# Threshold attention and a tanh-shrink layer on one core: all later k and q turned by the DMA crossbar, loads issued by ScalarE

## The chip, the core and the metric

The kernel runs on one core of a Trainium2 chip. The metric is the device time of one execution in microseconds (us), as the median over several runs. The core has a matrix engine (TensorE, PE in the profile, with its weight loads as PEld), VectorE (DVE), ScalarE (ACT), GpSimd (POOL) and a sync engine (SP) that only issues DMAs. Each of them works through its own instruction stream in order, and they wait for each other by semaphores. Sixteen DMA engines move the data; SP and ACT can both hand work to them. A DMA can also transpose 2-byte data on its way ("crossbar transpose").

## The reference

Attention over 8 batches x 8 heads, 576 rows of 64 numbers each; scores that lie more than `tau` below their row's maximum are dropped. A two-layer block follows, without a bias:

```python
scores = (1 / sqrt(64)) * q @ k.T                 # per batch and head, 576 x 576
thresh = max(scores, -1) - tau
scores = where(scores >= thresh, scores, -1e9)
attn = exp(scores - max(scores)); attn /= sum(attn) + 1e-9
x = (attn @ v), heads side by side                # 4608 x 512
h = x @ w_in                                      # 4608 x 2048
out = (h - tanh(h)) @ w_out                       # 4608 x 512, float32
```

## The kernel before

**Tiling.** Two heads of one batch make a pair; there are 32 pairs, four to a batch. A pair has nine score tiles of 128 query rows by 576 keys: four for each head and a ninth that holds the last 64 rows of both heads. So there are 288 tiles. The main loop runs over slots `s`, one tile wide: in slot `s` the scores of tile `s + 8` are made (AHEAD is 8), the threshold step `kink` is made for tile `s + 5`, the exponentials (`weights`) for tile `s`, and the product with v (`attend`) for tile `s - 2`.

**Preparing k and q.** q and k arrive in float32 (`load`, L137 to L153: a 256 KB piece for rows 0 to 511 of both heads, and a 32 KB piece for the last 64 rows, both on SP). POOL's `split` (L189 to L193) scales them and writes a high and a low fp16 half side by side, `hl`. These must be turned so that the 64 numbers of a row stand on the partitions: `turn` (L252). On PE that is nine transposes (L240) into one buffer of the two-buffer PSUM pool `ps_big`, which the scores also use, and one copy by DVE to `kT` or `qT` (L268). From pair 8 on, q of three pairs out of four goes another way: one crossbar transpose, issued by SP (L257), writes `qT` directly. For k, POOL then copies the two halves of the partitions into each other's place, `kS` (L274). The scores are sums of products with `kT` and with `kS` (L336; L327 for the shared ninth tile). `MAIN` and `REM` name the columns of a head's 512 first and 64 last keys.

**From the scores on.** DVE scales them out of PSUM and takes the row maximum (L346, L358); ACT makes the thresholded difference `z` (L373). In the first six pairs PE transposes z and ACT takes the exponentials from PSUM (L392, L401); from then on SP has z of two tiles turned by the crossbar (L380) and ACT takes the exponentials of both at once (L409). PE multiplies with v (L432, L439, L450), DVE divides, PE turns the result into `xT` (L482, L488, copied by L495 and L496).

**The second block.** When a batch's four pairs are through, its 512-row block goes through the two layers while the next batch's attention runs. An `h` step is four matmuls into `psH` (L505), then tanh on ACT (L518) and the difference on DVE (L524). A `y` step is four matmuls into `psY` (L531); every fourth one is copied out by DVE (L544) and stored by SP (L547). Which slot has an `h`, a `y` or nothing is written by hand in a string of 36 characters per batch, `PATTERN`, with 16 `h`, 16 `y` and four empty slots in the middle batches. The last 64 rows of all batches are gathered in `xR` and done in the end, after the attention.

**What sets the order.** The order is written out by hand. Each preparing step of pair `p` is put a number of slots ahead of the slot in which the pair's first scores are made:

```python
first = TPP * p - AHEAD                     # TPP = 9 tiles a pair
plan.setdefault(first - d, []).append(...)  # d: slots ahead
```

In before, k, q and v of a middle pair are loaded some 12 to 17 slots ahead, k is split 8 and q 7 to 10 slots ahead, k is turned 6 slots ahead, and q 6 or 7 by the crossbar and 2 by PE. Within a slot the plan's steps come last. Raw buffers, `hl`, `kT`, `qT` and `kS` have two copies each, so a step also waits until the pair two before it no longer needs its buffer.

Of the kernel before, what the change touches and what calls it, by code (L numbers as in the profile page):

```python
# [9 lines left out]
F32 = mybir.dt.float32  # L10
BF16 = mybir.dt.bfloat16
FP16 = mybir.dt.float16
# [6 lines left out]
def kernel(  # L19
# [11 lines left out]
    nc = tc.nc  # L31
    P = 128
# [13 lines left out]
    HPAIR = H // 2  # L46
# [85 lines left out]


    raws = {}

    def load(p, t):
        b, h0 = p // HPAIR, 2 * (p % HPAIR)
        hs = slice(h0, h0 + 2)  # L140
        src = {"k": k, "q": q, "v": v}[t]
        eng = nc.sync
        r = raws[p, t] = raw_pool.tile([P, 10, D], F32, name=f"{t}raw", tag=t)
        n = 8 if t == "v" else 10
        eng.dma_start(
            out=r[:, 0:n, :].rearrange("p (h c) d -> p h (c d)", h=2)[:, :, 0 : 4 * D],
            in_=src[b, hs, 0:512, :].rearrange("h (p c) d -> p h (c d)", c=4),
        )
        rem = src[b, hs, 512:S, :].rearrange("h s d -> s h d")
        if t == "v":  # L150
            eng.dma_start(out=r[0:64, 8:10, :], in_=rem)
        else:
            eng.dma_start(out=r[:, 4, :], in_=rem)  # L153

    def load_first(t, h, eng):

        src = {"k": k, "q": q}[t]
        if (0, t) not in raws:
            raws[0, t] = raw_pool.tile([P, 10, D], F32, name=f"{t}raw", tag=t)
        r = raws[0, t]  # L160
        if h is None:
            rem = src[0, 0:2, 512:S, :].rearrange("h s d -> s h d")
            eng.dma_start(out=r[:, 4, :], in_=rem)
        else:
            eng.dma_start(
                out=r[:, 5 * h : 5 * h + 4, :].rearrange("p c d -> p (c d)"),
                in_=src[0, h, 0:512, :].rearrange("(p c) d -> p (c d)", c=4),
            )
# [17 lines left out]
    def split(p, t):  # L186
        x = raws.pop((p, t))[:, 0:9, :]
        hl = hl_pool.tile([P, TPP, 2, D], FP16, name=f"{t}hl", tag=t)
        nc.gpsimd.tensor_scalar(  # L189
            out=x, in0=x, scalar1=QKSC, scalar2=1.0, op0=ALU.mult, op1=ALU.mult  # L190
        )
        nc.gpsimd.tensor_copy(out=hl[:, :, 0, :], in_=x)
        nc.gpsimd.tensor_tensor(  # L193
            out=hl[:, :, 1, :], in0=x, in1=hl[:, :, 0, :], op=ALU.subtract
        )
        hls[p, t] = hl
# [21 lines left out]

    def split_v(p):
        r, vb = raws.pop((p, "v")), vbs[p % NV]  # L220
        nc.gpsimd.tensor_copy(
            out=vb[:, :, 0:4, 0:D],
            in_=r[:, 0:8, :].rearrange("p (h c) d -> p h c d", h=2),
        )
        nc.gpsimd.tensor_copy(out=vb[0:64, :, 4, 0:D], in_=r[0:64, 8:10, :])
        nc.gpsimd.tensor_copy(out=vb[64:P, :, 5, 0:D], in_=r[0:64, 8:10, :])

    mats = {}  # L230


    by_head = lambda ap: ap.rearrange("p (s h) -> p h s", h=2)
    in_heads = lambda ap: ap.rearrange("p (h s) -> p h s", h=2)

    def turn_chunk(out, c, lhsT):
        rhs = ident_f16
        if c == 4:
            out, rhs = in_heads(out), by_head(rhs)
        nc.tensor.matmul(  # L240
            out=out, lhsT=lhsT, rhs=rhs, is_transpose=True, start=True, stop=True
        )
# [5 lines left out]

    def q_by_dma(p):

        return p >= 2 * HPAIR and p % 4 != 0

    def turn(p, t):
        hl = hls.pop((p, t))
        if t == "q" and q_by_dma(p):
            m = mats[p, t] = qk_pool.tile([P, W], FP16, name=f"{t}T", tag=t)
            nc.sync.dma_start_transpose(  # L257
                out=m.rearrange("p (c r) -> p c r", c=TPP),
                in_=hl.rearrange("p c a d -> p (c a d)"),
            )  # L260
            return
        ps = ps_big.tile([P, W], FP16, name=f"ps_{t}", tag="big")
        for c in range(TPP):
            turn_chunk(
                ps[:, c * P : (c + 1) * P], c, hl[:, c, :, :].rearrange("p a d -> p (a d)")
            )
        m = qk_pool.tile([P, W], FP16, name=f"{t}T", tag=t)
        nc.vector.tensor_copy(out=m, in_=ps)  # L268
        mats[p, t] = m
        if t == "k":  # L270
            sw = qk_pool.tile([P, W], FP16, name="kS", tag="ks")
            for lo, hi in ((0, D), (D, 0)):
                o, i = sw[lo : lo + D, :], m[hi : hi + D, :]
                nc.gpsimd.tensor_copy(out=o, in_=i)  # L274
            mats[p, "ks"] = sw

    def turn_first(t, part):

        hl = hls[0, t[0]]
        c0, c1 = ((0, 5), (5, TPP))[part]  # L280
        pl, tag = (ps_y, "y") if t == "ks" else (ps_h, "h")
        ps = pl.tile([P, 5 * P], FP16, name=f"ps1_{t}", tag=tag)
        for c in range(c0, c1):
            o = ps[:, (c - c0) * P : (c - c0 + 1) * P]
            if t == "ks":
                for a in range(2):
                    turn_chunk(o[64 * a : 64 * a + 64, :], c, hl[:, c, 1 - a, :])
            else:
                turn_chunk(o, c, hl[:, c, :, :].rearrange("p a d -> p (a d)"))
        if part == 0:  # L290
            mats[0, t] = qk_pool.tile([P, W], FP16, name=f"{t}T", tag=t)
        dst, n = mats[0, t][:, c0 * P : c1 * P], (c1 - c0) * P
        if part == 1 or t == "q":
            nc.scalar.copy(out=dst, in_=ps[:, 0:n])
        else:
            nc.vector.tensor_copy(out=dst, in_=ps[:, 0:n])


    MAIN = (slice(0, 512), slice(640, W))
    REM = (slice(512, 576), slice(576, 640))  # L300
    scs, mxs, nbs, zs, zts, pts, ops = {}, {}, {}, {}, {}, {}, {}

    def kind(i):
# [9 lines left out]
    def scores(i):  # L313
        p, hh, t = place(i)
        qT, kT, kS = mats[p, "q"], mats[p, "k"], mats[p, "ks"]
        ps = ps_big.tile([P, 1024], F32, name="psS", tag="big")
        main, rem, lo = slice(0, 512), slice(512, 576), 0
        if kind(i) == "B":
            main, rem, lo = slice(512, 1024), slice(448, 512), 448
        if hh is None:  # L320
            qrem = REM
            if q_by_dma(p):
                qrem = (slice(512, 640, 2), slice(513, 640, 2))
            for n, kk in enumerate((kT, kS)):
                for dst, srcs in ((main, MAIN), (rem, REM)):
                    for hh in range(2):
                        nc.tensor.matmul(  # L327
                            out=ps[64 * hh : 64 * hh + 64, dst],
                            lhsT=qT[:, qrem[hh]], rhs=kk[:, srcs[hh]],
                            start=(n == 0), stop=(n == 1),  # L330
                        )
        else:
            lhs = qT[:, (5 * hh + t) * P : (5 * hh + t + 1) * P]
            for n, kk in enumerate((kT, kS)):
                for dst, src in ((main, MAIN[hh]), (rem, REM[hh])):
                    nc.tensor.matmul(  # L336
                        out=ps[:, dst], lhsT=lhs, rhs=kk[:, src],
                        start=(n == 0), stop=(n == 1),
                    )
        sc = sc_pool.tile([P, S], F32, name="sc")  # L340
        if kind(i) == "B":
            mx = mxs[i] = mxs.pop(i - 1)
        else:
            mx = mxs[i] = mx3[i // 2 % len(mx3)]
        c = int(kind(i) == "B")
        nc.vector.tensor_scalar(  # L346
            out=sc, in0=ps[:, lo : lo + S], scalar1=SC, scalar2=None,
            op0=ALU.mult, op1=ALU.max, accum_out=mx[:, c : c + 1],
        )
        scs[i] = sc  # L350
# [163 lines left out]
    def bend():  # L514
        while halves:
            m, n, ps = halves.pop(0)
            th = t_pool.tile([P, MB], F32, name="th")
            nc.scalar.activation(out=th, in_=ps, func=ACT.Tanh)  # L518
            ths.append((m, n, ps, th))

# [8 lines left out]
    def project(m, ms, part, ps, last, cols=slice(0, d_model)):  # L529
# [4 lines left out]
            )  # L534
        if part == 3:
            nc_ = cols.stop - cols.start
            yo = y_pool.tile(
                [P, nc_], F32, name="yo", tag="yo" if nc_ == d_model else f"yo{int(last)}",
                bufs=2 if nc_ == d_model else 1,
            )  # L540
            if last:
                nc.scalar.copy(out=yo, in_=ps)
            else:
# [16 lines left out]
    EARLY = lambda m: 3 if m else 3  # L560
    LAST = 1

    PATTERN = lambda m: '-h--h-hh--h-hh-h-hh-h--hh-h--hh-y-yy' if m == 0 else 'hyhyhyhyhyhyhyhyhyhyhyhyhyhyhyhy' if m == B - 2 else 'yhyhyyy-yhyhhyyhy-hhhyhh-hyhyhy-yhhy'

    FIRST = 3
    quarters = lambda m: [(m, ms, part) for ms in range(4) for part in range(4)]
# [112 lines left out]
    )  # L679

    plan = {}
    for p in range(1, NPAIR):
        first = TPP * p - AHEAD
        for d, f in PREP[3 if p == 1 else 0 :]:
            d -= p == 1 and d == 3
# [150 lines left out]
```

## Time and profile before

| what | value |
|---|---|
| median of 9 runs | 518.06 us (518.0 to 518.22) |
| the profiled execution | 518.0 us, its span 516.2 us |
| PE busy | 501.7 us (97% of the span) |
| ACT busy | 433.0 us (84%) |
| DVE busy | 419.2 us (81%) |
| POOL busy | 289.9 us (56%) |
| DMA moved | 86.79 MB, mean 168 GB/s |
| crossbar transposes | 117 of z, 18 of q |

"Busy" is the time in which an engine works on an instruction; issuing DMAs and waiting don't count. The span runs from the first to the last instruction of the profiled execution, and the time of that execution is 1.8 us longer than the span. A share over the whole span mixes three stages: up to about 115 us (start, the first pairs, weights being loaded), the long middle up to about 421 us in which attention and layers run side by side, and an end of layers alone. The slices of the page show them, each digit the busy share of one fortieth of the span in tenths:

```profile
PE   8999899889999999999999999999999999999997
...
ACT  5999999999899989998999989998999899543430
...
DMA  6852669899998999999999998999979976311013
```

### The profile page before, as it was taken

How to read it: one execution, taken by the hardware profiler on the slowest of the kernel's cores; microseconds unless marked ns; L12 is line 12 of the kernel's file. 1: busy time of each engine (PE TensorE's matmuls, PEld its weight loads, DVE VectorE, ACT ScalarE, POOL GpSimd, SP SyncE). 2: the span in 40 equal slices, each digit the busy share in tenths (PEclk: the TensorE clock that was granted, in tenths of full speed). 3: DMA queues.
4: the chain of work that ended last, by engine and by line, in shares of the span. 5: the costliest groups of instructions: out<-in, count | busy, mean ns of one | idle time of the engine just before them, and what ended most of it. 6: DMA issues, size and time to landing. Idle time of an engine off the chain costs nothing.

```text
span 516.2 us, 12692 instructions
## 1 busy us (share of the span) xinstructions
PE 501.7 (97%) x4606; PEld 284.8 (55%) x4606; DVE 419.2 (81%) x1179; ACT 433.0 (84%) x617; POOL 289.9 (56%) x390
## 2 busy tenths in 40 slices
PE   8999899889999999999999999999999999999997
PEld 4666566555555555555555555555555555544444
DVE  5899889998899988998899888998999887644440
ACT  5999999999899989998999989998999899543430
POOL 7999999776565656566666656566656620000000
PEclk9999999999999999999999999999999999999999
DMA  6852669899998999999999998999979976311013
GB/s 213 252 151 90 208 194 230 162 189 187 200 197 172 210 207 199 177 192 215 209 164 200 202 206 195 185 200 207 204 162 194 174 140 116 98 41 42 20 43 82
DMA packets 208607, 86.79 MB, mean 168 GB/s; under 512 B 176160, under 2 KB 200992, under 8 KB 208544
## 3 DMA queue, kind: packets, MB, share of 16 engines
q1 hardware_dynamic: 207952, 85.56, 78.9%
q8 instruction: 36, 0.59, 0.5%
q10 hardware_dynamic: 592, 0.43, 0.3%
q14 instruction: 27, 0.22, 0.1%
HBM read 36.70 MB, written 9.44 MB: 89 GB/s over the span
## 4 chain that ended last, share of the span: by engine, by line
PE 79%; POOL 10%; ACT 3%; DVE 3%; issue 2%; DMA 1%; SPq 0%; POOLq 0%; ACTq 0%; DVEq 0%
PE psY L531 23%; PE psH L505 20%; PE psS L336 18%; PE psO L439 5%; PE psS L327 3%; PE psHt L505 3%; PE ps_k L240 2%; POOL kS L274 2%; POOL w_in_sb L655 1%; PE psO L450 1%; POOL khl L193 1%; PE psO L432 1%; DVE sc L346 1%; PE psX L482 1%; ACT z L373 1%
## 5 line engine op out<-in xcount | busy, mean ns | idle before, releaser
L373 ACT ACTIVATE z<-sc,nb 128x576 bf16<-128x576 f32 x288 | 217.7, 770 | 23.5 <-DVE nb L358 21.6
L346 DVE TENSOR_SCALAR_CACHE_REDUCE sc<-psS 128x576 f32<-128x576 f32 x288 | 213.5, 751 | 17.6 <-PE psS L336 13.5
L531 PE MATMUL psY<-w_out_sb,g 128*128 128x512 bf16 (+1 forms) x592 | 145.7, 373 | 0.0
L409 ACT ACTIVATE pT<-zT 128x1152 f16<-128x1152 bf16 x117 | 134.8, 1152 | 1.9 <-DMA zT<-z 1.6
L274 POOL COPY kS<-kT 64x1152 f16<-64x1152 f16 x62 | 70.7, 1141 | 109.6 <-DVE nb L358 58.4
L505 PE MATMUL psH<-xT,w_in_sb 128*128 128x512 bf16 x480 | 123.4, 379 | 1.0 <-DVE g L524 0.6
L336 PE MATMUL psS<-kT,qT 128*128 128x512 f16 (+1 forms) x512 | 104.4, 285 | 4.5 <-DVE sc L346 2.4
L336 PEld LDWEIGHTS <-qT 128*128 128x128 f16 x1024 | 72.9, 97 | 56.5 <-issue 5.3
L524 DVE SCALAR_TENSOR_TENSOR g<-th,psH 128x512 bf16<-128x512 f32 x128 | 87.4, 683 | 18.3 <-ACT th L518 18.0
L336 PE MATMUL psS<-kS,qT 128*128 128x512 f16 x496 | 101.4, 286 | 0.0
L518 ACT ACTIVATE th<-psH 128x512 f32<-128x512 f32 x128 | 74.6, 583 | 20.9 <-PE psH L505 20.9
L531 PEld LDWEIGHTS <-g 128*128 128x128 bf16 x592 | 51.1, 98 | 54.1 <-DVE g L524 0.4
L505 PEld LDWEIGHTS <-w_in_sb 128*128 128x128 bf16 x576 | 49.0, 98 | 56.3 <-issue 3.4
L439 PE MATMUL psO<-vb,pT 128*128 128x65 bf16 x1024 | 53.3, 194 | 0.0
L439 PEld LDWEIGHTS <-pT 128*128 128x128 f16 x1024 | 44.2, 98 | 9.4
L193 POOL TENSOR_TENSOR khl<-kraw,khl 128x576 f16<-128x576 f32 x31 | 39.7, 1280 | 2.7
L193 POOL TENSOR_TENSOR qhl<-qraw,qhl 128x576 f16<-128x576 f32 x31 | 39.7, 1280 | 2.7
L401 ACT ACTIVATE pT<-psZ 128x512 f16<-128x512 bf16 (+1 forms) x54 | 35.1, 653 | 2.8 <-PE psZ L392 2.5
L544 DVE COPY yo<-psY 128x512 f32<-128x512 f32 (+1 forms) x31 | 21.1, 681 | 14.7 <-PE psY L531 13.8
L465 DVE TENSOR_TENSOR osb<-psO,rc 128x256 bf16<-128x256 f32 x64 | 27.2, 424 | 2.2
L432 PE MATMUL psO<-vb,pT 128*128 128x130 bf16 x128 | 28.1, 220 | 0.0
L268 DVE COPY kT<-ps_k 128x1152 f16<-128x1152 f16 x31 | 23.4, 755 | 4.5 <-PE ps_k L240 4.3
(79 smaller groups left out, 508.4 us busy)
## 6 DMA issues: line engine op xcount, KB each, us to landing
vraw<-in_v_dram SPq DMA_DIRECT2D x32, 256.0 KB, 3.5
out_dram<-yo SPq DMA_DIRECT2D x32, 256.0 KB, 2.9
kraw<-in_k_dram SPq DMA_DIRECT2D x31, 256.0 KB, 3.3
qraw<-in_q_dram SPq DMA_DIRECT2D x31, 256.0 KB, 3.5
wt<-in_moe_w_in_dram SPq DMA_DIRECT2D x8, 512.0 KB, 4.4
wt<-in_moe_w_out_dram SPq DMA_DIRECT2D x8, 512.0 KB, 4.3
zT<-z SPq DMA_TRANSPOSE x117, 3.6
qraw<-in_q_dram SPq DMA_DIRECT2D x32, 32.0 KB, 3.1
```

The lines of the kernel that those rows point to most:

```text
L193: nc.gpsimd.tensor_tensor(out=hl[:, :, 1, :], in0=x, in1=hl[:, :, 0, :], op=ALU.subtract)
L274: nc.gpsimd.tensor_copy(out=o, in_=i)
L336: nc.tensor.matmul(out=ps[:, dst], lhsT=lhs, rhs=kk[:, src], start=(n == 0), stop=(n == 1),)
L346: nc.vector.tensor_scalar(out=sc, in0=ps[:, lo : lo + S], scalar1=SC, scalar2=None, op0=ALU.mult, op1=ALU.max, accum_out=mx[:, c : c + 1],)
L373: nc.scalar.activation(out=z, in_=sc, func=ACT.Prelu, bias=nb, scale=1.0, alpha=STEEP)
L401: nc.scalar.activation(out=pt[:, off * P : (off + n) * P], in_=ps[:, 0 : n * P], func=ACT.Exp)
L409: nc.scalar.activation(out=pt[:, 0 : n * P], in_=zts.pop(i)[:, 0:n, :], func=ACT.Exp)
L439: nc.tensor.matmul(out=po[:, t - 1 + ab, :], lhsT=pt[:, blk * P : (blk + 1) * P], rhs=vb[:, hh, c, :], start=False, stop=(n == 7), skip_gr ...
L505: nc.tensor.matmul(out=ps, lhsT=w_in_sb[:, c, n * P : (n + 1) * P], rhs=xs[m][:, c, :] if m < B else xR[:, c, :, :], start=(c == 0), stop= ...
L518: nc.scalar.activation(out=th, in_=ps, func=ACT.Tanh)
L524: nc.vector.scalar_tensor_tensor(out=gs[m][:, n, :], in0=th, scalar=-1.0, in1=ps, op0=ALU.mult, op1=ALU.add,)
L531: nc.tensor.matmul(out=ps, lhsT=gs[m][:, n, ms * P : (ms + 1) * P], rhs=w_out_sb[:, n, cols], start=(n == 0), stop=(n == DF_C - 1),)
```

## The change

From pair 8 on (`DUAL = 8`):

- **Turning.** k and q of every pair are turned by a crossbar transpose on SP (`q_by_dma`, `k_by_dma`). Before, PE turned every k, and q of every fourth pair. `kS` is still made by POOL, now in a step of its own, `swap`.
- **Loading.** `load_part` loads k in one DMA of 128 x 2304 bytes, in which a partition holds nine neighbouring rows of one head (partitions 0 to 63 the first head, 64 to 127 the second). q and v take two DMAs each: q as before in a 256 KB and a 32 KB piece, v in two halves by partitions, nine neighbouring rows to a pair of partitions. The five DMAs are issued by ScalarE, spread over slots.
- **Keys in another order.** As a chunk of turned k now holds 64 keys of each head, `main_keys` and `rem_keys` pick one head's keys in runs of 64 columns; v is put in the same order.
- **Timing.** For these pairs the table `LATER` gives the slots ahead of each step: `k0`, `q0`, `v0`, `q1`, `v1` are the loads, `s` the splits, `t` the turns, `kw` the swap. Even and odd pairs have different numbers.
- **Layer pattern.** The middle batches have a new string with the same 16 `h`, 16 `y` and four empty slots.
- **Buffers.** A raw tile is twice as wide (for an option of loading two pairs at once, which `AT_ONCE = 1` leaves unused); two small output tiles at the end share the tanh buffers.

```diff
+    DUAL = 8
+    AT_ONCE = 1
+    LOADER = nc.scalar
...
+    def load_part(p, t, part):
...
+        if t == "k":
+            dst = both[:, :, 0:TPP, :].rearrange("p a c d -> p a (c d)")
+            rows = rows.rearrange("(a h) s d -> a (h s) d", h=2).rearrange(
+                "a (p c) d -> p a (c d)", c=TPP
+            )
+        elif t == "v":
+            rows = rows.rearrange("h (p c) d -> p h (c d)", c=TPP)
+            if part == 0:
+                dst, rows = heads[0:64, :, 0 : 4 * D], rows[:, :, 0 : 4 * D]
+            else:
+                dst, rows = heads[64:P, :, :], rows[:, :, 4 * D :]
+        elif part == 0:
+            dst = heads[:, :, 0 : 4 * D]
+            rows = rows[:, 0:512, :].rearrange("h (p c) d -> p h (c d)", c=4)
+        else:
+            dst = both[:, part - 1, 4, :]
+            rows = rows[2 * part - 2 : 2 * part, 512:S, :].rearrange("h s d -> s h d")
+        LOADER.dma_start(out=dst, in_=rows)
...
     def q_by_dma(p):
 
-        return p >= 2 * HPAIR and p % 4 != 0
+        return p >= DUAL
+
+    def k_by_dma(p):
+        return p >= DUAL
 
     def turn(p, t):
         hl = hls.pop((p, t))
-        if t == "q" and q_by_dma(p):
-            m = mats[p, t] = qk_pool.tile([P, W], FP16, name=f"{t}T", tag=t)
+        if (q_by_dma if t == "q" else k_by_dma)(p):
+            m = mats[p, t] = qk_tile(t)
             nc.sync.dma_start_transpose(
-                out=m.rearrange("p (c r) -> p c r", c=TPP),
+                out=m[:, 0:W].rearrange("p (c r) -> p c r", c=TPP),
                 in_=hl.rearrange("p c a d -> p (c a d)"),
             )
             return
...
+    def swap(p):
+        m = mats[p, "k"]
+        sw = qk_tile("ks")
+        for lo, hi in ((0, D), (D, 0)):
+            o, i = sw[lo : lo + D, 0:W], m[hi : hi + D, 0:W]
+            nc.gpsimd.tensor_copy(out=o, in_=i)
+        mats[p, "ks"] = sw
...
+    def main_keys(p, kk, hh):
+        if p < DUAL:
+            return kk[:, MAIN[hh]]
+
+        return kk[:, 0 : 8 * P].rearrange("p (a n r) -> p n a r", a=2, n=4)[
+            :, :, :, 64 * hh : 64 * hh + 64
+        ]
...
-    PATTERN = lambda m: '-h--h-hh--h-hh-h-hh-h--hh-h--hh-y-yy' if m == 0 else 'hyhyhyhyhyhyhyhyhyhyhyhyhyhyhyhy' if m == B - 2 else 'yhyhyyy-yhyhhyyhy-hhhyhh-hyhyhy-yhhy'
+    PATTERN = lambda m: {
+        0: '-h--h-hh--h-hh-h-hh-h--hh-h--hh-y-yy',
+        B - 2: 'hyhyhyhyhyhyhyhyhyhyhyhyhyhyhyhy',
+    }.get(m, 'h-yhyhhyhyyhyyhh-yhhyhhy-yhyyh-yyhhy')
...
+    LATER = {
+        0: (
+            ("k0", 17), ("q0", 15), ("v0", 13), ("kt", 7), ("q1", 15),
+            ("ks", 8), ("v1", 12), ("vs", 6), ("qs", 10), ("qt", 7),
+            ("kw", 3),
+        ),
+        1: (
+            ("k0", 19), ("v1", 14), ("q0", 18), ("v0", 16), ("qs", 11),
+            ("q1", 17), ("qt", 8), ("ks", 13), ("vs", 6), ("kt", 10),
+            ("kw", 7),
+        ),
+    }
+    for p in range(DUAL, NPAIR):
+        first = TPP * p - AHEAD
+        at = lambda d, f: plan.setdefault(first - d, []).append(f)
```

## The prediction

> **What bounds the kernel now.** I read the page first (busy shares, slices, DMA issues), then busy time per stretch, then the chain of waits inside one stretch, then the waits, and last the timeline around ACT's DMAs.
>
> The stretch table is the central view: one row per two pairs (18 score tiles, start of one shared tile to the start of the next but one), with columns length, then busy time of PE, PEld, DVE, ACT, POOL, clock, DMA share and GB/s.
>
> ```profile
> core 0: us, PE busy (x) PEld busy (x) DVE busy (x) ACT busy (x) POOL busy (x), PEclk, DMA share, GB/s
> ...
> 197.80:225.00 27.20, 27.17 (x261) 15.47 (x260) 25.23 (x71) 25.61 (x36) 16.37 (x22) 1.00 1.02 195
> 225.00:253.40 28.40, 28.40 (x261) 15.85 (x262) 24.77 (x74) 26.17 (x36) 18.10 (x24) 1.00 1.01 201
> ...
> 421.00:444.00 23.00, 22.41 (x196) 12.21 (x197) 17.22 (x49) 20.97 (x29) 0.00 (x0) 1.00 0.62 125
> ```
>
> From 114.6 to 391.8 us there are ten such rows, 27.72 us each on average. PE is never idle in them, ACT is busy 25.77 on average (its ten rows lie between 25.36 and 26.17), DVE about 25.0. So PE sets the pace and ACT has only 1.95 us of room. The chain of waits in one stretch (start, length, what) says the same, and prices the work to be removed:
>
> ```profile
> 230.70 0.49 PE psS L336 x4
> 231.19 0.86 PE psY L531 x4
> 232.05 0.50 PE ps_k L240 x9
> 232.56 0.49 PE psS L336 x4
> ```
>
> Turning one k or q on PE is nine transposes in 0.50 us of the chain. (The group's busy time, 0.67, overlaps its neighbours; I use the chain's.) In this stretch every piece of the chain is PE. Who waits for what, from 197.8 to 308.9 us:
>
> ```profile
> ACT z L373 <- DVE nb L358: 6.7, 12, 0.8
> DVE sc L346 <- PE psS L336: 2.7, 4, 0.7
> ...
> ACT pT L409 <- DMA zT<-z: 0.4, 1, 0.4
> ```
>
> ACT waits for scores that PE has not yet made, 1.7 us per two pairs, and hardly ever for a crossbar transpose. The DMA issues of the same stretch (us to landing at the end):
>
> ```profile
> kraw<-in_k_dram SPq DMA_DIRECT2D x8, 256.0 KB, 3.0
> ...
> zT<-z SPq DMA_TRANSPOSE x37, 3.6
> ...
> qT<-qhl SPq DMA_TRANSPOSE x6, 3.4
> ```
>
> and, from the start of the kernel, the only mid-size loads that ACT issues:
>
> ```profile
> 0.73 0.65 ACTq L163 DMA_DIRECT2D kraw<-in_k_dram  x1
> ...
> 1.42 1.16 ACTq L165 DMA_DIRECT2D qraw<-in_q_dram  x2
> ```
>
> 0.58 to 0.65 us of ACT's instruction stream for each, while SP issued its own beside them.
>
> [...] No run here has large loads on ACT beside transposes. [...] The start of the trace shows two issuers at once with only about 0.1 us added (0.65 and 0.67 for 32 KB loads against a median of 0.565 on SP alone); beside a transpose it is not shown. [...]
>
> **The change, part by part.**
>
> *Turns leave PE and DVE.* For pairs 8 to 31, all 24 k turns and the 6 q turns that PE still did (every fourth pair) go: 30 x 0.50 = 15.0 us of PE chain. The changed program has 540 fewer PE instructions, which is 270 transposes with their weight loads. With them go 30 DVE copies of 755 ns, 22.7 us, 1.9 per two pairs, on an engine that was not the bound. Their two-buffer PSUM pool is then the scores' alone, which can only help. Per two pairs PE loses 2 k and half a q: 2.5 x 0.50 = 1.25, so its floor is 27.72 - 1.25 = 26.47.
>
> *What is late next.* ACT, with 25.77 of 26.47, 97%. DVE falls to about 23.1. Two engines that close, each in order and feeding the other, don't both run full: bounds are nothing lost (15.0 gained) and ACT keeping two thirds of its old idle time (1.3 us, so 27.07 per two pairs and 0.65 x 12 = 7.8 gained). I take a loss of 0.25 per two pairs: 1.0 x 12 = 12 us. After 426 us the chain already runs through ACT, which is a reason not to take the whole 15.
>
> *Transposes on SP.* 30 more, so 13 instead of 10.5 per two pairs. SP's issue time was 10.5 x 1.41 (median of zT) + 12 loads x 0.56 + 2 stores x 0.54 = 22.6 of 27.7; it becomes 13 x 1.41 + 1.1 = 19.4 of 26.5. So SP has more room. Its in-order waits are new: a kT or qT waits for POOL's split and the last reader of the buffer, and behind it stand zT transposes that ACT's exp waits for. By the plan, splits come one to three slots ahead and POOL has time to run ahead (16 to 18 us busy of 27.7). An odd pair's k and q each fall between two zT; an even pair's fall in one slot, and 3 x 1.41 = 4.2 us of issue meets two slots of 2.9 us, so the next zT is 1.3 us late. zT is asked for five slots after its input, about 7.3 us, and lands in 3.6: covered by about 2.4 us. Cost nothing; if landing grew by 3 us the cover would be gone and ACT would stall on it.
>
> *kS on POOL.* The swap (two copies of 1.14 us) now waits for a landed transpose rather than DVE. Even pairs: transpose 7 slots, swap 3 slots before the first score; 4 slots are 5.9 us against 3.4 to landing plus up to 2.8 of queue. Done about 1.4 slots ahead; nothing, with a few tenths a pair at risk.
>
> *Loads on ACT.* [...] They write buffers that POOL freed at least eight slots before, and most follow an activation of 0.77 to 1.15 us. [...] I take nothing; the lower bound is nothing too, because ACT issues almost none now, and the upper bound is all of it.
>
> *DMA traffic.* 2.5 more transposes per two pairs; k goes from 1 KB runs to 2.3 KB ones. The share of 1.0 looks full, but it goes above 1.0 in some stretches, so it counts packets that wait for each other; landing times near their minimum (zT 3.2 minimum, 3.6 median) say there is room. Cost nothing.
>
> *Moving operand in 64-column runs* (keys of both heads interleaved), and the *new layer pattern* (still 16 h, 16 y, 4 empty slots): same column counts. Strided reads by PE are not in the trace at this width; I take nothing, bound 10% below.
>
> **Sum.** Against the profiled execution, 518.0 us (span 516.2): 518.0 - 12 = 506.0, and the runs' median, 518.06, is 0.06 from it. Predicted 506, its own range 501 to 512.
>
> **Rivals.**
> - *ACT pays for its issues* (the slower side). Place: ACT's stream, pairs 8 to 31. Price: 5.7 us per two pairs times the exposed part. It decides from 1.95 / 5.7 = 34% exposed, where ACT alone needs the old 27.72. At half exposed: 25.77 + 2.85 = 28.62, 0.9 x 12 = 11 longer: 529. [...] Chance 0.19.
> - *DMA becomes the bound.* If 1.0 means full, 2.5 x 1.41 = 3.5 us more per two pairs, less about 1 for longer runs: 30 us longer, 548; half of that 533. Against: landings near their minimum. 0.08.
> - *Strided keys slow the score matmuls.* A score tile is the four matmuls of 0.49 us in the chain: 24 pairs x 9 tiles x 0.49 = 106 us; 8% slower costs 8: 514. For it: never run before. Against: the runs are whole 128-byte pieces. 0.10.
> - *No visible change* because ACT's room is less than it looks: 0.03.
>
> **Numbers.** Likeliest 0.60. Two per mille, 1 us, is what a measurement here can tell. Faster: 0.60 + most of the strided case, 0.69; same 0.04; slower 0.27. Range 500 to 527 leaves out a little below and the deeper half of the slow cases.
>
> **What would show it.** Right: no PE transposes after pair 7, two-pair stretches near 26.7 us, ACT above 95% busy, exp waiting for zT hardly more than now, ACT's DMA issues beside running activations. Wrong: ACT idle with "issue" or with a load ahead of it; zT landing at 6 us or more with ACT waiting; x4 score groups above 0.49 in the chain; PE waiting for kS.

## The result, and the profile after

| what | before | after |
|---|---|---|
| runs | 518.0 to 518.22 us, median 518.06 (31) | 508.9 to 521.73 us, median 513.48 (10) |
| the profiled execution | 518.0 us, span 516.2 | 508.9 us, span 507.1 |
| PE instructions, DVE instructions | 4606, 1179 | 4336, 1149 |
| zT, from issue to landing, min/median/max | 3.2 / 3.6 / 5.9 us | 3.2 / 4.6 / 8.8 us |

The change makes the kernel faster: the ratio is 0.9873 (0.9859 to 0.9887 at 95%), which stands for 518.06 x 0.9873 = 511.5 us. That ratio leaves out the four of the ten executions that were over 1.5% above the fastest, though the kernel before had none of that kind; with them in, the mean is 514.8 us. Two things came out of it: a gain of about 6.6 us by the ratio (3.2 by the mean of all ten), and a time that no longer repeats. The runs before lie within 0.2 us of each other, those after within 13.

The page of the kernel after: busy time by engine, DMA by slice, two of the queues (packets, MB, share of 16 engines' time), the chain that ended last, and the loads that ScalarE now issues (KB, us to landing).

```profile
PE 488.7 (96%) x4336; PEld 270.3 (53%) x4336; DVE 399.2 (79%) x1149; ACT 432.2 (85%) x617; POOL 291.1 (57%) x390
...
DMA  7852658999999999999999999999999976211013
...
q1 hardware_dynamic: 213520, 73.17, 75.1%
q10 hardware_dynamic: 20944, 21.67, 16.5%
...
PE 60%; POOL 11%; DMA 9%; ACT 7%; DVE 6%; issue 4%; ACTq 1%; SPq 1%; POOLq 0%
...
kraw<-in_k_dram ACTq DMA_DIRECT2D x24, 288.0 KB, 4.7
```

The fifth of these lines, the chain that ended last, is the one to read first. The same line of the kernel before:

```profile
PE 79%; POOL 10%; ACT 3%; DVE 3%; issue 2%; DMA 1%; SPq 0%; POOLq 0%; ACTq 0%; DVEq 0%
```

PE's own work has become shorter, as intended, and pieces of DMA, ACT and DVE now stand in the chain between its instructions. The 20,944 packets on the second queue, q10, are ScalarE's loads.

The stretch table again, four stretches of two pairs each (columns as before: length, busy time of PE, PEld, DVE, ACT, POOL, clock, DMA share, GB/s).

```profile
166.00:193.70 27.70, 27.43 (x243) 14.79 (x242) 23.76 (x70) 27.34 (x38) 19.25 (x25) 1.00 1.19 244
193.70:220.90 27.20, 26.11 (x235) 14.04 (x234) 22.61 (x67) 24.05 (x34) 15.89 (x21) 1.00 1.23 214
220.90:249.80 28.90, 28.14 (x243) 14.97 (x244) 24.12 (x72) 26.98 (x37) 17.85 (x23) 1.00 1.20 220
249.80:275.70 25.90, 25.82 (x234) 14.07 (x234) 22.91 (x68) 25.08 (x36) 17.58 (x23) 1.00 1.20 244
```

The ten stretches of the long middle last 27.3, 25.6, 27.7, 27.2, 28.9, 25.9, 27.3, 26.4, 28.5 and 25.6 us. Those without a stall alternate between 27.3 and 25.6, a mean of 26.45. The others run up to 1.6 us over: in the second row above PE is idle for 1.1 of 27.2 us and ACT for 3.2. The last columns changed too: the DMA share, 1.01 and 1.02 in the two rows of the middle shown before, is 1.19 to 1.23.

Who waits for whom in the whole span of the kernel after (us in total, times, longest):

```profile
POOL kS L323 <- DMA kT<-khl: 51.6, 15, 5.2
...
ACT pT L469 <- DMA zT<-z: 10.2, 11, 2.5
...
POOL kraw L225 <- DMA kraw<-in_k_dram: 6.0, 5, 2.2
```

ACT's wait for zT over the whole span of the kernel before:

```profile
ACT pT L409 <- DMA zT<-z: 1.6, 3, 0.9
```

The first line of the three above looks worst and is mostly harmless: POOL's swap waited for k before the change as well, 49.6 us in 12 times, and POOL has time.

One such stall close up, in the timeline (start, us, what; "x3" of the first row is three issues in a row, 9.00 us from the first's start to the last's end; the bracket is the engine's idle time and its releaser):

```profile
219.61 9.00 SPq L440 DMA_TRANSPOSE zT<-z  x3
...
219.90 0.76 ACT L433 ACTIVATE z<-sc,nb 128x576 bf16<-128x576 f32 x1
...
220.07 0.39 ACTq L172 DMA_DIRECT2D kraw<-in_k_dram  x1
...
227.90 0.67 POOL L225 TENSOR_SCALAR kraw<-kraw 128x576 f32<-128x576 f32 x1 [2.16 <-DMA kraw<-in_k_dram]
228.05 1.16 ACT L469 ACTIVATE pT<-zT 128x1152 f16<-128x1152 bf16 x1 [1.35 <-DMA zT<-z]
```

ScalarE issues a load of k at 220.07, beside an activation of its own that runs from 219.90 to 220.66: the issue, 0.39 us, costs ACT nothing, as its next activation starts at 220.57. The transfer takes 7.68 us in the chain of waits. In the same 9 us SP gets no more than three transposes issued, in 2.1, 3.0 and 3.1 us where the median is 1.45. At the end POOL has stood 2.16 us for k, and ACT 1.35 us for zT. Neither of these two engines was short of time. What their transfers have in common are the 16 DMA engines; whether those are what ran short, the experiments have to tell.

### The profile page after: what moved, and what is told of

The parts are those of the page before. It is cut to its first block, busy times and chain, and to the rows that moved or that the text cites. A ratio compares the mean times of both kernels' runs of the same rounds, so it can differ in the third digit from the quotient of the medians.

```text
span 507.1 us, 12208 instructions
## 1 busy us (share of the span) xinstructions
PE 488.7 (96%) x4336; PEld 270.3 (53%) x4336; DVE 399.2 (79%) x1149; ACT 432.2 (85%) x617; POOL 291.1 (57%) x390
## 2 busy tenths in 40 slices
DMA packets 234525, 95.61 MB, mean 189 GB/s; under 512 B 205152, under 2 KB 223840, under 8 KB 234464
## 3 DMA queue, kind: packets, MB, share of 16 engines
q10 hardware_dynamic: 20944, 21.67, 16.5%
## 4 chain that ended last, share of the span: by engine, by line
PE 60%; POOL 11%; DMA 9%; ACT 7%; DVE 6%; issue 4%; ACTq 1%; SPq 1%; POOLq 0%
PE psY L591 20%; PE psH L565 15%; PE psS L396 13%; DMA zT<-z 4%; PE psO L499 3%; ACT z L433 3%; POOL kS L323 3%; PE psHt L565 3%; DVE g L584 3%; ACT pT L469 2%; DVE sc L406 2%; DMA kraw<-in_k_dram 2%; ACT th L578 2%; PE psS L387 2%; POOL w_in_sb L717 1%
## 5 line engine op out<-in xcount | busy, mean ns | idle before, releaser
L469 ACT ACTIVATE pT<-zT 128x1152 f16<-128x1152 bf16 x117 | 135.2, 1156 | 10.8 <-DMA zT<-z 10.2
L396 PE MATMUL psS<-kS,qT 128*128 128x512 f16 (+1 forms) x512 | 104.6, 286 | 0.3 <-POOL kS L323 0.3
L525 DVE TENSOR_TENSOR osb<-psO,rc 128x256 bf16<-128x256 f32 x64 | 27.2, 424 | 2.2
L225 POOL TENSOR_SCALAR qraw<-qraw 128x576 f32<-128x576 f32 x31 | 20.8, 670 | 10.5 <-DMA qraw<-in_q_dram 8.9
```

The costliest lines, as they stand in the source:

```text
L396: nc.tensor.matmul(out=ps[:, dst], lhsT=lhs, rhs=cols(p, kk, hh), start=(n == 0), stop=(n == 1),)
L469: nc.scalar.activation(out=pt[:, 0 : n * P], in_=zts.pop(i)[:, 0:n, :], func=ACT.Exp)
```

## The experiments

The gain could have fallen short of the 15.0 us of PE time in four ways: ACT pays for its issues; two nearly full engines rub against each other, which is what the forecast had taken; transposes and loads crowd the DMA engines; or the lateness is one of order, and more slack cures it. Diffs are against the kernel after. Ratios are to the kernel before.

**The same issues with less to move.** All 120 loads of ScalarE stay where they are; from pair 10 on each moves about a quarter of its bytes, q's last rows apart, into raw tiles of its own. What isn't loaded is left from earlier pairs, and POOL's scaling there multiplies by 1.

```diff
+        if p >= DUAL + 2 and t == "k":
+            dst, rows = dst[:, :, 0 : 2 * D], rows[:, :, 0 : 2 * D]
+        elif p >= DUAL + 2 and (t == "v" or part == 0):
+            dst, rows = dst[:, :, 0:D], rows[:, :, 0:D]
```

> The changed kernel with the same 120 DMA issues on ACT, but from pair 10 on k, q and v loads move only about a quarter of the bytes (k 2 of 9 chunks, q and v one of four or five); the rest of the data is left from earlier pairs. Traffic theory (loads and transposes crowd the 16 DMA engines, so transposes land late and exp waits): runs near 504 to 506 us, lying within about 1 us of each other instead of 13, zT landing back to 3.6 to 4.0 us median, exp's wait for zT under 3 us. Issue theory (ACT pays for issuing loads): no change, about 511 with the same scatter. Close-engines theory (PE and ACT at 97% disturb each other): no change.

Measured: median 503.45 us (502.64 to 505.0), ratio 0.9719 (0.9706 to 0.9732). Two stretches of it, and the landing of zT:

```profile
141.60:167.20 25.60, 25.28 (x231) 13.99 (x234) 23.09 (x68) 24.73 (x35) 18.54 (x25) 1.00 0.98 179
167.20:194.50 27.30, 26.98 (x239) 14.75 (x242) 23.77 (x70) 26.70 (x37) 18.04 (x23) 1.00 1.07 182
```

```profile
DMA to landing us min/median/max: 3.2/3.5/8.4
```

Between 141 and 273 us its chain of waits is PE's again, with 1.2% for anything else:

```profile
by line: PE psS L404 29.7%; PE psH L573 25.8%; PE psY L599 25.7%; PE psO L507 7.7%; PE psS L395 4.2%; PE psO L518 2.2%; PE psO L500 1.7%; PE psX L550 1.7%; issue 1.2%; PE psX L556 0.2%
```

This run settles two theories at once. 14.6 of the 15.0 us come through with every issue of ScalarE in place, so the issues cost next to nothing. And they come through with ACT 97 to 98% busy (24.73 of 25.60, 26.70 of 27.30), so these two nearly full engines didn't rub. Only bytes were taken away, and the loss went with them. The trace has as many DMA packets as that of the kernel after, 234,525, so it isn't their number.

**Fewer transposes, full loads.** The same question from the other side: two of nine crossbar transposes of z in every two pairs are left out.

```diff
+            if DUAL * TPP <= i and i % 18 in (1, 11):
+                zts[i] = zt_last[0]
+                return
```

> The changed kernel with two of the nine zT transposes of every two pairs left out from pair 8 on (those tiles' exponentials read the zT turned before); PE, ACT, DVE, POOL and all loads do what they did. By uncontended packet times the DMA engines are asked for 23.1 of 26.45 us per two pairs in the changed kernel, 20.1 in the run with short loads, 20.2 of 27.7 before, and 20.5 here. If only the sum of the traffic counts: 503 to 505.5, scatter under 3 us, as with short loads. If it is loads from a second queue beside transposes that collide, whatever the sum: 507 to 513 with several us of scatter.

Measured: 504.09 us (503.77 to 506.11), ratio 0.974 (0.9726 to 0.9755). The chain between 141 and 273 us:

```profile
by line: PE psS L397 29.7%; PE psY L595 26.2%; PE psH L569 25.9%; PE psO L503 7.7%; PE psS L388 5.0%; PE psO L514 2.2%; PE psO L496 1.7%; PE psX L546 1.7%; PE psX L552 0.2%
```

PE alone. Loads of full length with fewer transposes do what short loads with all transposes do. So neither the loads nor the transposes are the trouble by themselves: taking from either is enough, as it would be if their sum counted. As all loads from DRAM are still there, DRAM alone isn't it. One thing this run leaves open: it also takes two of thirteen transposes out of SP's stream of instructions. The zT that are left land in 4.1 us at the median, half a microsecond above the kernel before, and still PE doesn't stand in this stretch: this longer landing is covered.

**All loads back on SP.**

```diff
-    LOADER = nc.scalar
+    LOADER = nc.sync
```

> The changed kernel with the loads of pairs 8 to 31 issued by SP instead of ACT, in the same slots. Traffic theory: SP's stream is nearly full (13 x 1.45 + 10 x 0.5 + 1.1 = 25 us of 26.5 per two pairs), transposes queue behind loads: 513 us or more. Issue theory: ACT gets its stream back, 503 to 507. Close-engines theory: about the same as the change, 511.

Measured: 530.39 us (530.01 to 531.81), ratio 1.0242 (1.0229 to 1.0255): slower than before the change. zT lands well, in 3.7 us at the median and 6.1 at the longest, and yet exp waits for it:

```profile
ACT pT L469 <- DMA zT<-z: 32.7, 29, 2.9
```

So here the lateness comes before the issue: from 120 to 400 us SP's DMA issues take 93% of its time, 85% in the middle of the kernel after. The queue on ScalarE is a needed part of the change, not a detail of it.

**Only v on SP.** Two of the five loads of a pair go back, which makes ScalarE's queue shorter.

```diff
-        LOADER.dma_start(out=dst, in_=rows)
+        (nc.sync if t == "v" else LOADER).dma_start(out=dst, in_=rows)
```

> The changed kernel with v's two loads issued by SP, k's and q's by ACT. The bytes are the same. If the sum counts: 509 to 514, same scatter; SP's stream is asked for 13 x 1.4 + 4 x 0.6 + 1.1 = 21.7 of 26.45 us. If loads from a second queue collide with transposes: a third fewer collisions, 507 to 510. If SP's stream is what runs out, as with all loads on it (530): 514 to 522.

Measured: 526.78 us (526.01 to 527.41), ratio 1.0167 (1.0153 to 1.0181), a miss for every theory in size; the direction is that of SP running out. SP's instruction stream in the timeline:

```profile
200.45 0.65 SPq L172 DMA_DIRECT2D vraw<-in_v_dram  x1
201.20 1.40 SPq L440 DMA_TRANSPOSE zT<-z  x1
202.65 1.08 SPq L172 DMA_DIRECT2D vraw<-in_v_dram  x1
203.82 4.36 SPq L440 DMA_TRANSPOSE zT<-z  x2
208.28 1.30 SPq L301 DMA_TRANSPOSE kT<-khl  x1
```

Each row starts within 0.1 us of the end of the one before, and a transpose takes 1.3 to 2.2 us to issue in these rows. From 130 to 400 us SP's issues take 94% of its time. Thirteen transposes at the 1.45 us that the kernel after needs are 18.9 of 26.5 us; four loads of v at 0.65 to 1.1 us and the stores don't fill the rest at the median, but they do once the transposes slow down.

**k back on PE, loads left on ScalarE.**

```diff
     def k_by_dma(p):
-        return p >= DUAL
+        return False
```

> The changed kernel with k turned by PE again in all pairs, q all by the crossbar, loads on ACT. PE floor: 24 turns of 0.50 us come back, 6 of the 30 stay away: 518 - 3 = 515. Traffic theory: 7.5 to 9 fewer transposes out of 13 per two pairs only takes 2, that is enough to land zT at 3.6 to 4.0 us again: 515 with a scatter under 1 us. Issue theory: 516 to 520 with several us of scatter, since all loads are still issued by ACT. Close-engines theory: 515 without scatter, as ACT has its room again.

Measured: 518.97 us (518.22 to 520.01), ratio 1.0016 (1.0008 to 1.0025), some 4 us above what was expected. A piece of its chain:

```profile
212.44 0.52 PE ps_k L281 x9
213.05 0.77 DVE kT L313
213.86 0.65 PE psS L396 x4
```

The turn is back, and in this arrangement PE also stands behind DVE's copy of it (6 times, 2.6 us in all), which it didn't in the middle of the kernel before. Why the copy now comes in the way wasn't followed up. What the run does show: the new loads, with q's last six turns off PE, bring nothing by themselves, so the gain hangs on k's turns. And its runs scatter by 1.8 us only, though zT lands in 4.5 us at the median; the wait of exp for it is 1.4 us in 4 times. In packets (206,109 against 208,607) and bytes (88.54 MB against 86.79) this traffic is about that of the kernel before, where zT landed in 3.6 us. So the sum of the traffic doesn't set the landing alone; the loads from a second queue may be what lengthens it, which no run separates, and here the longer landing stays covered.

**More slack at zT.** One slot more between the scores and the use of zT.

```diff
-    AHEAD = 8
+    AHEAD = 9
-    MASK = 5
+    MASK = 6
-        at = i - 4 if i < HPAIR * TPP else i
+        at = i - 5 if i < HPAIR * TPP else i
```

> The changed kernel with every score, z and preparing step one slot earlier than the exponentials (AHEAD 9, MASK 6), so that a zT has six slots to land instead of five. Traffic theory: exp's wait for zT goes (10 us to under 2), runs 506 to 509 with a scatter under 3 us, with up to 1.5 us of it being the added slot. Issue theory and close-engines theory: unchanged or 1.5 longer, 511 to 513, with the same scatter.

Measured: median 517.5 us (509.37 to 524.36, 22 runs), ratio 0.9924 (0.9904 to 0.9943): no better. The middle also starts later in its trace (121.4 us against 113.1), so the time alone tells little. The chain does:

```profile
173.69 6.74 DMA kraw<-in_k_dram
...
180.94 8.35 DMA kT<-khl
...
190.62 1.15 POOL kS L323
...
191.81 0.64 PE psS L396 x2
```

exp's wait for zT falls, but only from 10.2 to 6.8 us. With zT given more slack, the lateness arrives by the other road: a load of k of 6.7 us, a transpose of 8.4 us, the swap, and PE stands until the swap is done.

**More slack for k and the loads.** Loads two to four slots earlier; the even pairs' split and turn of k two or three slots earlier; both together. The core of the first two edits (the even pairs' turn itself moves from 7 to 9 slots):

```diff
-            ("k0", 17), ("q0", 15), ("v0", 13), ("kt", 7), ("q1", 15),
+            ("k0", 21), ("q0", 19), ("v0", 16), ("kt", 7), ("q1", 19),
...
-            ("ks", 8), ("v1", 12), ("vs", 6), ("qs", 10), ("qt", 7),
-            ("kw", 3),
+            ("ks", 11), ("v1", 12), ("vs", 6), ("qs", 9), ("qt", 7),
+            ("kw", 5),
```

> The changed kernel with k's and q's loads four slots (about 6 us) and v's two to three slots earlier, transposes where they are. Late-load form of the traffic theory (a load that lands after 7 instead of 4 us delays the split, the turn and kS): 505 to 508, scatter under 4 us, POOL's waits for loads gone. Crossbar form (what lands late is zT and kT, whose issue slows to 3 us each beside any load): 509 to 514 as before, since as many loads meet as many transposes.

> The changed kernel with an even pair's k split at 11 instead of 8, turned at 9 instead of 7 and swapped at 5 instead of 3 slots ahead (q split at 9 instead of 10), so that no two turns fall in one slot. Crossbar form of the traffic theory: the pile of three transposes in two slots (4.2 us of issue against 2.9) goes and kS has two slots more: 506 to 509 with less scatter. Late-load form: no gain, or worse, since the split of k now has six slots after its load instead of nine: 511 to 516.

> Both of these edits together. If lateness of a few us is all that the traffic does, slack at both places takes it up: 504 to 507, scatter under 2 us, near the run with short loads (503.5). If the engines are simply too full, slack is used up in a while and 509 to 514 stays.

Measured: loads earlier 516.9 us (512.02 to 521.55, 22 runs), ratio 0.9966 (0.9952 to 0.998); k's turn earlier 513.57 (511.02 to 517.44), 0.9922 (0.9892 to 0.9952); both 516.47 (511.58 to 519.98), 0.994 (0.9914 to 0.9966). None gains, and earlier loads lose most; with them exp's wait for zT is 16.2 us. Asking earlier for the same traffic didn't make room here. Why it costs time is not settled.

**The layer pattern of before.**

```diff
-    }.get(m, 'h-yhyhhyhyyhyyhh-yhhyhhy-yhyyh-yyhhy')
+    }.get(m, 'yhyhyyy-yhyhhyyhy-hhhyhh-hyhyhy-yhhy')
```

> The changed kernel with the middle batches' layer pattern of before. Traffic theory: the pattern moves h and y steps by a slot or two and is no matter for the DMA engines, same floor of 26.45 us per two pairs, 509 to 514 with the same scatter. If the pattern is what lets PE reach its floor: undisturbed two-pair stretches above 26.45, 514 us or more.

Measured: 513.22 us (507.85 to 515.96), ratio 0.9886 (0.9852 to 0.992), which overlaps the change's own interval. No effect of the pattern can be told.

**Some q back on PE.** A mix that trades a little PE time for less traffic: q of every fourth pair, then of every second.

```diff
     def q_by_dma(p):
-        return p >= DUAL
+        return p >= DUAL and p % 4 != 0
```

> The changed kernel with q of every fourth pair turned by PE as before, so 12.5 instead of 13 transposes per two pairs and 0.25 us more of PE: floor 503.5 + 6 x 0.5 = 506.5. If the sum counts, a step from 23.1 to 22.4 us asked for takes away a part of the stalls: 508 to 512, less scatter, no clear gain over the change. If every transpose more or less counts little: 511 to 515.

> The changed kernel with q of every second pair turned by PE, so 12 transposes per two pairs: the DMA engines are asked for 21.8 us of 26.95 (81%; 87% in the changed kernel, 78% and 76% in the two quiet runs). PE floor 503.5 + 12 x 0.5 = 509.5. If the sum counts: 509.5 to 511 with a scatter under 3 us, so it is steadier than the change and its median a little lower, though not its best run. If 81% is still too much: 511 to 515 with several us of scatter.

Measured: 510.4 us (508.2 to 512.69), ratio 0.9856 (0.983 to 0.9881), and 511.68 us (509.61 to 513.11), ratio 0.9882 (0.9863 to 0.99). Both intervals overlap the change's. exp waits less for zT, 6.2 and 3.5 us in all against 10.2, so the traffic is eased; the runs, only five and four, scatter by 4.5 and 3.5 us. The turns on PE eat what that brings. No version was found that clearly beats the change.

## Why the prediction was right, and where it was off

It said 506 us. The profiled execution took 508.9, the ratio stands for 511.5, and the median of all is 513.48. The direction held, and the first two lie in the range given for the likeliest case, 501 to 512; the median of all lies only in the wide one. Step by step:

- **Turns leave PE: right.** 270 transposes went, and the stretches without a stall are 26.45 us on average where the sum gave 26.47. The two kernels with less traffic gained 14.6 and 14.0 of the 15.0 us.
- **"Two engines that close ... don't both run full", 3 us taken off: wrong.** With light traffic ACT ran at 97% and the chain was PE's but for 1.2%. No run shows such a loss; this term should have been nothing. That 506 came near is luck: the 3 us stood in for another loss, which the sum had priced at nothing.
- **"DMA traffic ... Cost nothing": the step that failed.** It is worth 511.5 - 503.45 = 8.0 us by the ratio, 514.8 - 503.65 = 11 by the means of all runs. The right sum is 15.0 gained, 0.4 lost elsewhere, 8.0 lost to traffic: 6.6. The argument was that landings near their minimum "say there is room". They said so of the traffic of before, not of 2.5 transposes more in a shorter stretch with two queues. The data for a better price was in the trace. At the median, a DMA packet of 256 bytes took 18 ns, one of 1 KB 46, one of 2 KB 84 and one of 2304 bytes 93. An estimate, which gives each packet of a stretch this length: the traffic asks for 73% of the 16 engines' time before (20.2 of 27.7 us), 87% after (23.1 of 26.45), 76% with short loads and 78% with fewer zT. The step should have set the first two side by side. In these runs and the mixes with q on PE, exp's whole wait for zT grows with this share: 1.6 us at 73%, 1.9 at 76, 2.6 at 78, 3.5 at 81, 6.2 at 84, 10.2 at 87. In the four runs that keep all the traffic and change the order or the pattern alone, without more slack at zT, it is 11.3 to 16.7.
- **Transposes on SP, "cost nothing; if landing grew by 3 us the cover would be gone": the condition came true.** The median landing grew by only 1.0 us, which the cover of 2.4 holds; the longest grew by 2.9 to 8.8, and exp stood for zT 11 times, 10.2 us in all, instead of 3 times and 1.6. A cover has to be set against the tail, not the median. Single long landings (up to 7.7 us) are there with fewer transposes too, but exp stood 5 times and 2.6 us there, and PE once for exp, 0.7 us.
- **"SP has more room": wrong.** The count made it 19.4 us of issue in 26.5, from medians. In the ten stretches of the trace SP's issues take 231 of 270 us, the 85% of before, though the loads are gone: 31 of the 130 transposes take over 2 us to issue, 5 of 105 did before. With short loads SP's issues take 75% of its time from 114 to 375 us, with fewer zT 69%. So these two runs ease the DMA engines and SP at once. That bytes set off the loss is shown; whether they act through slow issues on SP or through late landings after the issue isn't separated.
- **kS on POOL, "a few tenths a pair at risk": right in an ordinary stretch,** and in a bad one PE stood until the swap was done, 1.29 us of it at 191.81 in the run with more slack at zT.
- **Loads on ACT, nothing: right.** Short loads keep every issue and lose 0.4 us, so the rival in which ACT pays (529) falls. That price rests on 5.7 us a two pairs, ten issues at the 0.57 of SP's loads before; in the trace after, ten issues of ScalarE take 5.2 us by their medians (0.34 us for k, 0.51 for q, 0.61 for v). No run shows what hides them; what the runs show is the 0.4 us. Beside a transpose, an issue of ScalarE took 0.39 us within the 2.1 us in which SP issued the transpose.
- **Strided keys, nothing: right.** Four score matmuls in the chain take 0.49 us, as before the change.
- **DVE:** 30 copies fewer; its busy time fell by 20.0 us against 22.7 counted.
- **The rival "DMA becomes the bound"** (533 to 548) pointed to the traffic, rightly, but with the wrong law. It took the DMA share for a limit that adds its excess to every stretch. Instead, of the ten stretches in the profile after, four pay nothing and six pay 0.3 to 1.6 us, 5.9 us in all. What the queue on ScalarE brought was issue time, 15 to 19 us of it by the two kernels with loads on SP (526.78 and 530.39 less 511.5); the loss that stayed went where there was less to transfer (503.45 and 504.09).

What stays open: by which of the two roads the traffic delays zT and k, why earlier loads are worse, why k back on PE costs 4 us more than its turns, and what sets off a bad stretch. Moving the stores out of the crowded stretches wasn't tried.

## What to carry to other kernels

When work moves from an engine to DMA, add up the DMA engines' time that a stretch will ask for and set it against the new, shorter stretch. Here a time that repeated within 0.2 us and then scattered by 13 was the first sign that the shared DMA engines had come close to full, an estimated 87% of their time. With such a scatter one profile, which may be one of the better runs, tells too little by itself. To find out whether the traffic is the cause, leave every instruction in place and make only the transfers shorter.

## What the hardware showed that wasn't expected

- A pause of PE cost more than its length. In the run with more slack at zT (its profiled execution took 520.3 us), the stretch table in pieces of 4 us (columns as before) has PE idle for 2.4 us, and the granted clock drops afterwards, when PE is busy again:

```profile
188.00:192.00 4.00, 1.62 (x9) 0.60 (x8) 1.80 (x6) 2.60 (x4) 2.43 (x3) 0.96 0.96 205
192.00:196.00 4.00, 3.95 (x22) 1.93 (x22) 1.27 (x3) 2.27 (x4) 2.45 (x3) 0.61 1.03 201
```

  The chain of waits of the same run shows it in four like matmuls, during the low clock and a little later:

```profile
192.45 1.71 PE psH L565 x4
...
198.45 0.86 PE psH L565 x4
```

  The same work takes twice as long, so here a late transfer is paid for twice. Not every pause does this. In the run with q of every fourth pair on PE, 4 us (from 332 us) with PE busy for 2.47 were followed by four matmuls of an h step in 1.74 us, which take 1.03 at other times; in the run with v on SP, after 4 us (from 168 us) with PE busy for 2.45 the four matmuls of a y step took 1.02 us, no longer than at other times. What decides isn't shown.
- The DMA engines weren't full when they hurt. At an estimated 87% of their time asked for (the estimate above), the runs scattered by 13 us; at 76 to 78%, by 2.4 us, over five runs each. The landing alone doesn't tell: with k on PE, at about the traffic of before, the longest landing of zT was 8.2 us, against 8.8 in the kernel after, and exp waited 1.4 us.
